# First chunk's x put in place by TensorE in a linear-attention and MLP kernel

## The chip, the cores and the metric

The kernel runs on one core of one Trainium2 chip. A core has TensorE (matrix products, written to PSUM), VectorE (DVE), ScalarE (ACT), GpSimd (POOL) and SyncE (SP, which here only issues DMA transfers). The engines run their own instruction queues in order and wait for one another through semaphores. The metric is device time of one execution in microseconds, the median of several runs.

## The reference

Two blocks, all in float32. The first is a recurrent attention over 4 sequences, 8 heads, 768 steps and 40 channels per head, with a state matrix of 40 x 40 per sequence and head. The second is an MLP over the 3072 tokens, with 320 channels in and out and 2048 hidden ones.

```python
for t in range(S):
    y[:, :, t] = einsum('bhd,bhde->bhe', r_t, state)
    Sa = einsum('bhde,bhe->bhd', state, a_t)
    state = state * w_t[:, :, None, :] - einsum('bhd,bhe->bhde', Sa, b_t)
    state = state + einsum('bhd,bhe->bhde', v_t, k_t)
x = y.transpose(0, 2, 1, 3).reshape(B * S, H * D)
h = x @ w_in
out = (h * sigmoid(1.702 * h)) @ w_out
```

## The kernel before

**Units and chunks.** The 768 steps are cut into 12 chunks of 64. A unit i is one chunk (i // 2) for two of the four sequences (i % 2), so there are 24 units; all 16 heads of a unit are worked on together as 64 x 64 blocks, four at a time on the four quadrants of TensorE's array. A product in float32 is two weight loads and two matmul instructions in the trace; every matmul of the kernel has the same line there, L301, the helper `mm`, so products are told apart by the PSUM tile that they write.

**A unit's steps, with the names of their PSUM tiles.** The decays w are turned into logarithms by ACT. `cum` and `cumc` sum them over time, once with time and once with channels on the partitions (`cumc` serves the first four units only, `i < BY_PE`; later units get these sums from a scan on DVE). Exponentials of the sums scale a, b and k. `N`, `A` and `RV` are the score products. From N, five levels (`ps_level`, called L0 to L4 of a unit here) invert a triangular matrix by repeated squaring. In the first four units each level is one group of products, then a copy of 128 x 768 out of PSUM (PT, line 794) and a transpose (EX, line 733). `Q` and `T21` (the tile ps_T) finish the inverse; `B0` and `B1` gather the known terms; `X` solves (its product with the mask is M, line 917); `y` gives the outputs and the new state. From unit 2 on, `zT` and `rz` bring in the state of the unit two before. The last step is x = y times the decay (line 962).

**How x reaches the MLP.** The output of a unit has 40 channels of each head on the partitions, two heads side by side; the MLP's up product wants 64 rows of the 320 channels at a time. Before the change x goes to DRAM in two transfers (`part_with`) and comes back in two (`get_back`, one for each half of the partitions), into the tile xT_all.

**The MLP.** For each chunk, `up` multiplies x by w_in in four groups of 10 tasks (group q needs the q-th of eight weight pieces), ACT applies the gate, and `down` multiplies by w_out. An up task is four products of 256 columns; the 64 x 64 tiles are in w_sb.

**The weights** come in as 64-bit floats, in eight pieces of 1.3 MB, four transfers each, and are turned into 32-bit ones on the chip: ACT (line 457, "rebased"), three DVE passes (lines 461, 465, 469) and one on POOL (line 473, "joined").

**The order of the work.** The function does not issue instructions as it goes. It adds some 2700 tasks to a plan, and a list written out in the file, ORDER, gives the order in which they are issued. Each word is a task's number, a letter for the engine (p TensorE, a ACT, d DVE, g POOL, s SyncE) and a digit: for tasks with a PSUM tile the bank pair, for SyncE's how many transfers may be under way (it waits for the one that many back; without a digit it does not wait). An engine therefore takes its tasks in the listed order, whatever else is ready. TensorE's first 54 tasks, up to the first up task, are (unit in parentheses):

```
cum(0) cumc(0) RV(0) A(0) N(0) cumc(1) cum(1) L0(0) B1(0) RV(1) N(1) L1(0) B0(0) L0(1) L2(0) L1(1) A(1) L3(0)
cum(2) cumc(2) L2(1) L4(0) L3(1) Q(0) T21(0) N(2) L4(1) X(0) B1(1) y(0) Q(1) B0(1) L0(2) T21(1) A(2) cumc(3)
cum(3) X(1) zT(2) y(1) N(3) L1(2) RV(2) rz(2) L0(3) L2(2) B0(2) zT(3) B1(2) L3(2) L1(3) L4(2) RV(3) A(3) up
```

## Time and profile before

| | |
|---|---|
| median of 3 runs | 682.24 us (681.4 to 682.74) |
| profiled execution | 679.49 us, of it span 677.7 us |
| TensorE matmul busy | 649.6 us, 96% of the span |
| DVE, ACT, POOL busy | 449.7, 329.1, 175.7 us |
| granted TensorE clock, mean | 0.994 |
| transfers | 69.74 MB, mean 103 GB/s |
| first up product starts | 66.48 us |

The span runs from the first to the last instruction; the profiled execution's time is 1.8 us longer, for what lies around it. In the groups and the timeline a line shows an engine, the tiles written and read, the shape and the number of instructions, and in brackets how long the engine stood idle before it and what ended that. Busy time of TensorE includes the latency of products that stand alone, so a busy TensorE is not always one at its peak.

### The profile page before, as it was taken

Reading aid. Unit: us, or ns where it says so; the run is one execution under the profiler, and the core shown is the slowest. Engines: PE = TensorE matmul, PEld = TensorE weight load, DVE = VectorE, ACT = ScalarE, POOL = GpSimd, SP = SyncE. Lnnn points to the kernel's source line nnn. Section 1 sums busy time; section 2 is a strip of 40 time slices with the busy share of each in tenths; the row PEclk is TensorE's granted clock in tenths of the full one; section 3 lists DMA queues with packets and bytes.
Section 4 is the critical chain, followed back from the end, with each engine's and each line's share of the span. In section 5 each row is a group of like instructions: output and inputs, shape, how many; then the busy total and the mean of one; then the engine's idle time right before and its main releaser. Section 6 shows DMA issues by size and latency. Waiting matters only on the chain.

```text
span 677.7 us, 42447 instructions
## 1 busy us (share of the span) xinstructions
PE 649.6 (96%) x19616; PEld 568.7 (84%) x19616; DVE 449.7 (66%) x916; ACT 329.1 (49%) x681; POOL 175.7 (26%) x201
## 2 busy tenths in 40 slices
PE   5777999999999999999999999999999999999997
PEld 4667787787999997888888899999889798799896
DVE  5777779777867668757776687868656766675001
ACT  3676745634564655654545445455344454263010
POOL 6541443324123123123113211322411421300000
PEclk9979999999999999999999999999999999999999
DMA  6875753415324314432404513513412411200200
GB/s 208 295 255 160 226 172 97 129 42 152 107 64 131 94 58 124 114 107 65 124 14 131 149 35 108 155 33 107 140 38 62 130 53 45 69 15 14 60 13 21
DMA packets 35473, 69.74 MB, mean 103 GB/s; under 512 B 5472, under 2 KB 14816, under 8 KB 35296
## 3 DMA queue, kind: packets, MB, share of 16 engines
q1 hardware_dynamic: 35216, 66.99, 32.9%
q8 instruction: 154, 2.52, 1.6%
q14 instruction: 23, 0.19, 0.1%
q10 hardware_dynamic: 80, 0.04, 0.0%
HBM read 59.15 MB, written 7.86 MB: 99 GB/s over the span
## 4 chain that ended last, share of the span: by engine, by line
PE 88%; DMA 6%; DVE 2%; issue 1%; SPq 1%; ACT 1%; DVEq 0%; ACTq 0%
PE ps_up L301 31%; PE ps_down L301 29%; PE ps_level L301 8%; PE ps_y L301 5%; PE ps_B L301 4%; PE ps_X L301 2%; PE ps_N L301 2%; PE ps_rz L301 1%; PE ps_RV L301 1%; PE ps_A L301 1%; PE ps_zT L301 1%; SPq L331 1%; DMA w_sb<-in_w_in 1%; PE ps_cum L301 1%; PE ps_T L301 1%
## 5 line engine op out<-in xcount | busy, mean ns | idle before, releaser
L301 PE MATMUL ps_up<-xT_all,w_sb 64*64 64x256 f32 x3840 | 253.3, 377 | 2.1 <-issue 1.3
L301 PE MATMUL ps_down<-w_sb,g 64*64 64x320 f32 (+1 forms) x3200 | 241.5, 419 | 0.2 <-ACT zr L879 0.2
L301 PEld LDWEIGHTS ps_up<-xT_all,w_sb 64*64 64x64 f32 x3840 | 170.8, 133 | 18.8 <-issue 2.1
L301 PEld LDWEIGHTS ps_down<-w_sb,g 64*64 64x64 f32 x3200 | 142.5, 133 | 31.6 <-issue 0.4
L1000 ACT ACTIVATE g<-ps_up 128x1024 f32<-128x1024 f32 x48 | 49.2, 1025 | 46.3 <-PE ps_up L301 45.8
L719 POOL TENSOR_TENSOR EX<-ES,quads 128x512 f32<-128x512 f32 x30 | 39.7, 1324 | 116.4 <-DVE ES L712 77.7
L761 ACT COPY W<-ps_level 128x512 f32<-128x512 f32 x56 | 32.8, 585 | 67.7 <-PE ps_level L301 66.0
L301 PEld LDWEIGHTS ps_level<-W,EX 64*64 64x64 f32 x2560 | 60.0, 134 | 5.4 <-DVE T L840 0.2
L763 DVE TENSOR_TENSOR E<-two,ps_level 128x256 f32<-128x256 f32 x80 | 33.1, 415 | 36.5 <-ACT W L761 32.3
L301 PE MATMUL ps_level<-W,EX 64*64 64x64 f32 (+1 forms) x2560 | 56.8, 217 | 0.0
L717 ACT ACTIVATE EX<-ES,quads 128x256 f32<-128x256 f32 x82 | 37.2, 501 | 31.9 <-DVE ES L712 31.3
L629 POOL TENSOR_TENSOR ak<-ak,FT 128x512 f32<-128x512 f32 x17 | 23.0, 1353 | 77.2 <-DMA ak<-in_ak 54.4
L301 PEld LDWEIGHTS ps_level<-PT,EX 64*64 64x64 f32 x1280 | 30.7, 138 | 11.5 <-DVE EX L733 3.3
L301 PE MATMUL ps_level<-PT,EX 64*64 64x64 f32 (+2 forms) x1280 | 32.5, 234 | 6.9 <-DVE EX L733 5.0
L712 DVE STREAM_TRANSPOSE ES<-E 128x256 f32<-128x256 f32 x80 | 35.3, 443 | 4.4
L301 PE MATMUL ps_y<-RV,kh 64*64 64x104 f32 (+1 forms) x768 | 35.4, 247 | 0.9 <-DVE M L917 0.9
L301 PE MATMUL ps_y<-M,bh 64*64 64x104 f32 (+1 forms) x768 | 35.5, 247 | 0.7 <-DVE M L917 0.5
L901 ACT COPY B<-ps_B 128x416 f32<-128x416 f32 (+1 forms) x35 | 17.2, 493 | 34.4 <-PE ps_B L301 34.2
L301 PEld LDWEIGHTS ps_y<-RV,kh 64*64 64x64 f32 x768 | 29.6, 133 | 3.2 <-DVE M L917 1.5
L917 DVE TENSOR_TENSOR M<-ps_X,later 128x832 f32<-128x832 f32 (+1 forms) x24 | 23.9, 995 | 10.2 <-PE ps_X L301 10.0
L301 PE MATMUL ps_B<-RV,A 64*64 64x104 f32 (+1 forms) x768 | 29.2, 252 | 0.8 <-issue 0.8
L637 POOL TENSOR_TENSOR kh<-time,G 128x320 f32<-128x320 f32 x18 | 16.2, 901 | 51.2 <-PE ps_y L301 34.6
(133 smaller groups left out, 1099.0 us busy)
## 6 DMA issues: line engine op xcount, KB each, us to landing
ak<-in_ak SPq DMA_DIRECT2D x48, 160.0 KB
rv<-in_rv SPq DMA_DIRECT2D x48, 160.0 KB
time<-in_time SPq DMA_DIRECT2D x24, 320.0 KB
xT_all<-x_dram SPq DMA_DIRECT2D x48, 160.0 KB
wc<-in_wc SPq DMA_DIRECT2D x20, 264.0 KB
logw<-in_w SPq DMA_DIRECT2D x24, 160.0 KB
RV<-in_v SPq DMA_DIRECT2D x24, 160.0 KB
b<-in_b SPq DMA_DIRECT2D x48, 80.0 KB
```

The lines of the kernel that those rows point to most:

```text
L301: nc.tensor.matmul(o, lhsT, rhs, start=start, stop=True, skip_group_check=True)
L331: begun.append(queue.dma_start(dst, src).ins)
L629: plan.add(R, {"DVE": 690.0, "POOL": 1270.0, "sbuf": True}, lambda t: of(t.engine).tensor_mul(ahT(), ahT(), FT_of(i)), reads=T("ak", "FT") ...
L637: plan.add(R + 4, {"POOL": 870.0, "DVE": 490.0, "sbuf": True}, lambda t, n=n, dst=dst: of(t.engine).tensor_mul(dst(i)[:, :, :D], by_head(t ...
L712: plan.add(rank, dve(256), lambda t: nc.vector.transpose(ES(n), source(t)), writes=[key("ES", n, 6)], **reads)
L717: nc.scalar.activation(dst[:, :, h], ES(n), ACT.Copy, scale=quads[:, h, :1])
L719: of(t.engine).tensor_mul(dst, ES(n).unsqueeze(2).to_broadcast([128, 8, 2, 32]), quads.unsqueeze(1).to_broadcast([128, 8, 2, 32]))
L761: plan.add(rank, any2(512), lambda t: copy(t.engine)(tiles_of(W(n + 1)), blocks(psum(t, ""), 64)), writes=[key("W", n + 1, 5)], pair=pair)
L763: plan.add(rank, dve(256), lambda t: nc.vector.tensor_sub(tiles_of(E(n + 1)), every(two32, [128, 2, 4, 32]), blocks(psum(t, ""), 64)[:, :, ...
L901: plan.add(R, any2(4 * wide), lambda t: copy(t.engine)(dst(), some(psum(t, "")[:, :, :208])), writes=[("Bv", i)] if x and c > 0 else T("B" ...
L917: plan.add(R + 1, dve(8 * wide), lambda t: nc.vector.tensor_tensor(M_of(i)[:, :, :wide].rearrange("p (j b) n -> p b j n", b=2), some(psum( ...
L1000: plan.add(-45, {"ACT": 1030.0, "table": "gelu"}, lambda t: nc.scalar.activation(g_of(c * NQ + q).rearrange("p m r n -> p r m n"), psum(t, ...
```

## The change

For the two units of the first chunk x no longer goes through DRAM. TensorE multiplies it by a selection matrix (`first_sel`, 128 x 128, one product of 512 columns) for four of the five groups of 64 channels, and by four shifted slices of a second one (`rest_sel`) for the last, which accumulate four products of 128 columns; one copy brings the 640 columns from PSUM into xT_all. The two matrices are built at the start by a new task, `selections`. The channels of x and the rows of w_in get a new order, in all chunks; in the later chunks x still goes through DRAM, with four transfers back in place of two. For the first two units y times the decay is two DVE operations instead of four.

For the first four units the decays come in a copy in which each head has 64 columns (40 and 24 ones), 256 KB in place of 160, and `cumc` takes two heads at a time: 8 products with 128 columns of weights in place of 16 with 64. Three small memsets on POOL go.

ORDER is new throughout. TensorE's first 54 tasks are now (xp is the selection):

```
cumc(0) cum(0) N(0) A(0) cumc(1) cum(1) RV(0) L0(0) B0(0) N(1) L1(0) B1(0) L0(1) L2(0) A(1) L1(1) RV(1) L3(0)
cumc(2) cum(2) L2(1) L4(0) L3(1) Q(0) T21(0) L4(1) X(0) Q(1) N(2) y(0) B0(1) B1(1) cumc(3) cum(3) T21(1) L0(2)
xp(0) L1(2) X(1) N(3) A(2) y(1) zT(2) rz(2) RV(2) L2(2) xp(1) zT(3) B1(2) L0(3) L3(2) B0(2) L1(3) L4(2) up
```

SyncE's queue is in a new order too. Adding up the sizes of its transfers, the point by which each has been asked for is, in MB:

| landed with | before | after |
|---|---|---|
| b(0) / ak(0) | 1.31 / 0.82 | 0.75 / 1.08 |
| rv(0) | 1.15 | 2.49 |
| rv(1) | 2.62 | 5.44 |
| w(2) | 2.79 | 6.03 |
| last of weight 1 | 6.23 | 10.23 |
| rv(2) | 7.37 | 11.64 |
| last of weight 3 | 9.83 | 13.72 |

Up to the first up task in the list, DVE has 67 tasks before and 74 after, ACT 60 and 53, POOL 14 and 15, SyncE 54 and 48. The diff, with the two lists left out:

```diff
@@ ORDER: 2709 words replaced by 2710 @@
...
@@ -352,6 +352,7 @@
     make_identity(nc, full)
     ident = single("ident", [128, 64])
     nc.vector.tensor_add(ident, full[:, :64], full[:, 64:])
+    first_sel, rest_sel = single("first_sel", [128, 128]), single("rest_sel", [128, 132])
     one32, two32 = single("one32", [128, 32]), single("two32", [128, 32])
     nc.vector.tensor_add(one32, ident[:, :32], ident[:, 32:])
     nc.vector.tensor_add(two32, one32, one32)
@@ -372,9 +373,7 @@
         select(edges[q], ALU.is_gt, 0, 1, -1.0)
         select(edges[p.start + MID:p.stop], ALU.is_gt, -MID, 1, 0.0)
     incl = edges[:, 1:]
-    logw_t = several("logw", [128, DM + 24])
-    for t in logw_t:
-        nc.gpsimd.memset(t[:, DM:], 0.0)
+    logw_t = several("logw", [128, DM])
 
     quads, within = single("quads", [128, 2, 32]), single("within", [128, 2, 32])
     nc.gpsimd.memset(quads, 0.0)
@@ -493,12 +492,13 @@
     ak_of, b_of, rv_of = lambda i: ak_t[i % 2], lambda i: b_t[i % 2], lambda i: rv_t[i % 2]
 
     RV_of = lambda i: buf("RV", i, [128, 13, 8, 8])
-    logw_of = lambda i: logw_t[i % 3][:, :DM]
+    logw_of = lambda i: logw_t[i % 3] if i >= BY_PE else apart(i).rearrange("p (h d) -> p h d", h=H)[:, :, :D]
 
     wc_of = lambda i: buf("wc", i, [128, 2, 8 * 33])
+    apart = lambda i: wc_of(i).rearrange("p n h -> p (n h)")[:, :H * 64]
 
     def load_w(i):
-        for name, of, src, n in (("wc", wc_of, wc_d, 528), ("logw", logw_of, w_d, DM))[i < BY_PE:]:
+        for name, of, src, n in (("wc", wc_of, wc_d, 528), ("logw", logw_of, w_d, DM)) if i >= BY_PE else (("wc", apart, apart_d, H * 64),):
             plan.add(-2 if i == 2 else 10 * i - 30, {"SP": 350.0}, lambda t, of=of, src=src: transfer(t, of(i), src[i]),
                      writes=[(name, i)], size=128 * n * 4)
 
@@ -535,7 +535,7 @@
                 nc.scalar.activation(wc_of(i), wc_of(i), ACT.Ln)
             nc.scalar.activation(logw_of(i), logw_of(i), ACT.Ln)
         plan.add(10 * i - 30, {"ACT": 1000.0 if i >= BY_PE else 470.0, "table": "exp"}, go,
-                 reads=[("logw", i)] + ([("wc", i)] if i >= BY_PE else []) + ([("exps", i - 2)] if i > 1 else []), writes=[("log", i)])
+                 reads=[("wc", i)] + ([("logw", i)] if i >= BY_PE else []) + ([("exps", i - 2)] if i > 1 else []), writes=[("log", i)])
 
         def sums(t):
 
@@ -550,20 +550,20 @@
         R = 10 * i - 9
 
         def by_time(t):
-            ps, lw = psum(t, "ps_cum"), logw_of(i)
+            ps, lw = psum(t, "ps_cum"), logw_of(i) if i < BY_PE else logw_of(i).rearrange("p (h d) -> p h d", h=H)
             for n in (1, 0):
                 for b in BITS:
                     u = b ^ n
-                    mm(ps[HALF[u], b, :160], incl[HALF[b]], lw[HALF[b], n * 160:(n + 1) * 160], True)
-        plan.add(R, pe((1, 160)), by_time, reads=T("log"), uses=T("logw"), room=T("G"), writes=T("cum"), pair=("cum", i))
+                    mm(ps[HALF[u], b, :160].rearrange("p (h d) -> p h d", d=D), incl[HALF[b]], lw[HALF[b], 4 * n:4 * n + 4], True)
+        plan.add(R, pe((1, 160)), by_time, reads=T("log"), uses=T("logw") if i >= BY_PE else T("wc"), room=T("G"), writes=T("cum"), pair=("cum", i))
 
         def by_channel(t):
 
             ps = psum(t, "ps_cumc")
             for u, f in product(BITS, BITS):
-                for b, e in QUARTERS:
-                    o, h = (2 * u + f) * 65, head(e, f, b, u) * D
-                    mm(ps[HALF[e], b, o:o + 65], logw_t[i % 3][HALF[b], h:h + 64], edges[HALF[b]], o == 0)
+                for b in BITS:
+                    o, h = (2 * u + f) * 65, head(0, f, b, u)
+                    mm(ps[:, b, o:o + 65], apart(i)[HALF[b], 64 * h:64 * h + 128], edges[HALF[b]], o == 0)
 
         def exp_of_product(t):
             tables(t)
@@ -579,7 +579,7 @@
                     nc.scalar.activation(ends[:, n, b], sums[:, b, :, 64 * n].rearrange("p (u f) -> p u f", u=2), ACT.Exp, scale=2.0 * n - 1.0)
 
         if i < BY_PE:
-            plan.add(R, pe((4, 65)), by_channel, reads=T("log"), uses=T("logw"), room=T("FT", "GT"), pair=("cumc", i))
+            plan.add(R, pe_wide((4, 65)), by_channel, reads=T("log"), uses=T("wc"), room=T("FT", "GT"), pair=("cumc", i))
 
         def exp_channel(t):
             tables(t)
@@ -958,15 +958,24 @@
             x = x_of().rearrange("p (n f) b t -> p n b f t", f=2)
             for u, b in product(BITS, BITS):
                 at = slice(4 * u + 2 * b, 4 * u + 2 * b + 2)
-                y = both(i)[:, at, :64] if c > 0 else part(t)[:, u, 2 * b:2 * b + 2, :64]
-                of(t.engine).tensor_mul(x[:, b ^ u, b], y, FT_of(i)[:, at])
-        if c > 0:
-            plan.add(R + 6, {"DVE": 1200.0, "POOL": 2300.0, "sbuf": True}, decayed, reads=T("y", "FT"), uses=T("rz"), writes=T("x"))
-        else:
-            plan.add(R + 6, {"DVE": 1000.0}, decayed, reads=T("FT"), writes=T("x"), pair=("y", i))
-
-
-        rows = lambda: drams[i].rearrange("(e d j) n -> e d (j n)", e=2, d=D)
+                of(t.engine).tensor_mul(x[:, b ^ u, b], both(i)[:, at, :64], FT_of(i)[:, at])
+
+        def first_x(t):
+
+            x = x_of().rearrange("p (u f) b t -> p b u f t", f=2)
+            y, FT = (v.rearrange("p u (b f) t -> p b u f t", f=2) for v in (part(t)[:, :, :, :64], FT_of(i).rearrange("p (u j) t -> p u j t", u=2)))
+            for b in BITS:
+                nc.vector.tensor_mul(x[:, b, ::1 - 2 * b], y[:, b], FT[:, b])
+
+        def chosen(t):
+
+            ps = psum(t, "ps_xT")
+            nc.tensor.matmul(ps[:, 0], first_sel, x_of().rearrange("p j b t -> p (j b t)"), start=True, stop=True, skip_group_check=True)
+            for j in range(4):
+                nc.tensor.matmul(ps[:, 1, :128], rest_sel[:, 3 - j:131 - j], x_of()[:, j].rearrange("p b t -> p (b t)"),
+                                 start=j == 0, stop=True, skip_group_check=True)
+
+        rows = lambda: drams[i].rearrange("(d e j) n -> e d (j n)", e=2, d=D)
 
         def part_with(t):
             if i not in drams:
@@ -976,9 +985,19 @@
 
         def get_back(t):
             for h in HALF:
-                transfer(t, xT_of(c)[h, p].rearrange("q k n -> q (k n)"), drams[i].rearrange("(q k) n -> q (k n)", q=64))
-        plan.add(-50, {"SP": 700.0}, part_with, reads=T("x"), writes=T("xd"), size=DM * 512)
-        plan.add(-50, {"SP": 700.0}, get_back, reads=T("xd") + ([("weight", raws.index("x"))] if c in (1, 2) else []), writes=[("xT", c), ("xs", (c, p))], size=2 * DM * 512)
+                transfer(t, xT_of(c)[h, p, :4].rearrange("q k n -> q (k n)"), drams[i][:256].rearrange("(q k) n -> q (k n)", k=4))
+                transfer(t, xT_of(c)[h, p, 4], drams[i][256:])
+        if c > 0:
+            plan.add(R + 6, {"DVE": 1200.0, "POOL": 2300.0, "sbuf": True}, decayed, reads=T("y", "FT"), uses=T("rz"), writes=T("x"))
+            plan.add(-50, {"SP": 700.0}, part_with, reads=T("x"), writes=T("xd"), size=DM * 512)
+            plan.add(-50, {"SP": 2200.0}, get_back, reads=T("xd") + ([("weight", raws.index("x"))] if c in (1, 2) else []),
+                     writes=[("xT", c), ("xs", (c, p))], size=2 * DM * 512)
+        else:
+            plan.add(R + 6, {"DVE": 800.0}, first_x, reads=T("FT"), writes=T("x"), pair=("y", i))
+            plan.add(R + 7, {"PE": 1740.0, "instr": 20}, chosen, reads=T("x") + [("sel", 0)], pair=("xp", i))
+            plan.add(R + 7, any2(640), lambda t: copy(t.engine)(
+                xT_of(c)[:, p].rearrange("q k n -> q (k n)"), psum(t, "").rearrange("p r n -> p (r n)")[:, :640]),
+                     writes=[("xT", c), ("xs", (c, p))], pair=("xp", i))
 
 
     g_of = lambda n: buf("g", n, [128, 2, 2, 256])
@@ -1043,6 +1062,16 @@
         for p in BITS:
             down(p)
 
+    def selections(t):
+
+        of(t.engine).memset(first_sel, 0.0)
+        of(t.engine).memset(rest_sel, 0.0)
+        first = first_sel.rearrange("p (h d e) -> p h d e", h=2, e=2)
+        rest = rest_sel[:, 3:131].rearrange("p (h d e j) -> p h d e j", h=2, e=2, j=4)
+        for e in BITS:
+            for to, cols in (first[HALF[e], :, :, e], slice(0, 32)), (rest[HALF[e], :, :, e, 0], slice(32, D)):
+                of(t.engine).tensor_copy(to, ident[HALF[e], cols].unsqueeze(1).to_broadcast([64, 2, cols.stop - cols.start]))
+    plan.add(0, {"POOL": 1600.0, "DVE": 900.0}, selections, writes=[("sel", 0)])
     for i in range(3):
         load_w(i)
     for i in range(2):
@@ -1117,7 +1146,7 @@
         return n.reshape(*t.shape[:2], 2, 8 * 33)
 
 
-    order = [d + D * (e + 2 * j) for e in range(2) for d in range(D) for j in range(H // 2)]
+    order = [q // 2 + D * (q % 2 + 2 * k) if k < 4 else 32 + q // 8 + D * (q // 4 % 2 + 2 * (q % 4)) for q in range(64) for k in range(5)]
     def pieces(x):
 
         x = x.reshape(4, -1, *x.shape[1:]).transpose(0, 2, 1, 3)
@@ -1127,10 +1156,14 @@
     w_in = pieces(w_in.reshape(8, 128, 640))
     w_out = pieces(np.asarray(moe_w_out).reshape(16, 128, 320))
 
+    by_time = time_tile(w, False)
+    apart = np.ones((4, 128, H, 64), np.float32)
+    apart[..., :D] = by_time[:4].reshape(4, 128, H, D)
     arrays = {
         "in_time": np.ascontiguousarray(np.stack([time_tile(k, True), time_tile(b, True)], 2)),
         "in_v": beside(v),
-        "in_w": time_tile(w, False),
+        "in_w": by_time,
+        "in_apart": apart.reshape(4, 128, H * 64),
         "in_wc": halves(channel_tile(w, "e", "ubf")),
         "in_ak": np.ascontiguousarray(np.stack([channel_tile(a, "e", "ubf"), channel_tile(k, "e", "ubf")], 2)),
         "in_b": channel_tile(b, "e", "ubf"),
```

## The prediction

> **What bounds the kernel now.** I read the page's slices first, then the windows table, then the timeline of TensorE up to the first up product, then SyncE's issues. Slices of the whole span, 16.9 us each:
>
> ```profile
> PE   5777999999999999999999999999999999999997
> ...
> PEclk9979999999999999999999999999999999999999
> ```
>
> TensorE is full from the fifth slice on and has room only in the first four. The windows table gives that in us (window, length, then busy time of PE, PEld, DVE, ACT, POOL, granted clock, DMA share, GB/s):
>
> ```profile
> 10.00:20.00 10.00, 7.48 (x233) 6.73 (x229) 5.96 (x10) 2.98 (x11) 2.50 (x2) 1.00 0.80 255
> ...
> 30.00:40.00 10.00, 7.31 (x237) 6.53 (x239) 7.50 (x14) 7.52 (x23) 5.85 (x3) 0.75 0.93 311
> ...
> 60.00:70.00 10.00, 8.04 (x300) 7.07 (x304) 7.73 (x13) 6.58 (x15) 2.96 (x1) 1.00 0.50 146
> ...
> 120.00:640.00 520.00, 518.21 (x15848) 456.14 (x15844) 356.52 (x758) 253.09 (x511) 122.69 (x133) 1.00 0.30 87
> ```
>
> From 120 to 640 us only 1.8 us of 520 are idle; before the first up product some 21 of 66.5 are. So the end is set by how soon TensorE reaches that product with the same work behind it. The timeline (start, length) shows the steps on the way that I time below:
>
> ```profile
> 11.71 1.13 PE L301 MATMUL ps_N<-b,ak 40*64 40x64 f32 x32 [0.82 <-DVE b L631]
> ...
> 42.00 0.41 PE L301 MATMUL ps_y<-RV,kh 64*64 64x104 f32 x8 [0.91 <-DVE M L917]
> ...
> 64.82 0.67 PE L301 MATMUL ps_level<-PT,EX 64*64 64x32 f32 x32 [0.84 <-DVE EX L733]
> ...
> 66.02 0.65 PE L301 MATMUL ps_A<-ak 40*64 40x64 f32 x32
> 66.48 2.48 PE L301 MATMUL ps_up<-xT_all,w_sb 64*64 64x256 f32 x40
> ```
>
> N(0) starts at 11.7 because it waited for b and its product; y(0) at 42.0; L4(2), the last level of unit 2, at 64.8. Up then follows A(3) without idle time: **no wait for x shows there**. SyncE's issues say why: x left for DRAM late and came back just in time.
>
> ```profile
> 44.63 0.66 SPq L331 DMA_DIRECT2D x_dram<-x  x2
> ...
> 56.67 0.84 SPq L331 DMA_DIRECT2D x_dram<-x  x2
> 61.39 1.09 SPq L331 DMA_DIRECT2D xT_all<-x_dram  x2
> ```
>
> Unit 1's x is written by 53.3, and is asked back only at 61.4.
>
> **What stands ahead of the first up product.** Both orders put 54 TensorE tasks there, the same ones but for two: RV(3) and A(3) move behind it (0.47 us each in stream, starts 65.55, 66.02, 66.48), and the two selections come ahead. So the work behind is 677.7 - 66.5 = 611.2 us before and 612.1 after, and the change gains only if the first up product starts before 65.6.
>
> **The walk to it.** I go through the new order queue by queue, with durations from rows: a level 0.88 us of TensorE in stream (61.98 to 62.86), 0.25 more until its last result; ACT's PT copy 0.80 and DVE's transpose 0.71, one after the other, since DVE's EX waited 7.7 us in six waits on ACT's PT; X 0.71, M 1.02, y 1.5; a DVE pass over a weight 0.8, ACT's 1.42, POOL's 2.97. Bytes arrive at 240 GB/s up to 14 us (rows 190 and 255 in the first two windows) and at 300 from there (291, 311). Behind each step stands its start before.
> - The first load is 256 KB in place of 160: at the 275 GB/s of 2 to 4 us that is 0.4 us, and with a weight piece beside it up to 0.8. The logarithm starts at 3.5 (3.2), but cumc now leads cum, so the exponentials start at 4.75 (5.6).
> - b(0) and ak(0) now stand first in SyncE's queue (0.75 and 1.08 MB against 1.31 and 0.82), landed by 6.2. b, a and k are scaled by 8.2: N(0) at 7.5 (11.7).
> - RV(0) stands ahead of L0(0) and needs rv(0), 2.49 MB, 12.0: L0(0) 12.5 (14.9).
> - L1(0) is no longer behind RV(1): 15.6 (19.8). RV(1) holds L3(0) to its 5.44 MB: 22.9 (26.9). cumc(2) holds L4(0) until w(2) has landed at 24.3 and ACT took its logarithm: 26.9 (30.8).
> - Four crossed copies of 0.44 on DVE, then Q, T21, X(0): 32.0 (38.6). M, then y(0): 34.6 (42.0).
> - L0(2) 37.8 (45.2), the first selection 38.7 to 40.4. ACT's first pass over weight 1 stands ahead of exp(3) and of the PT copy for L1(2); its last piece is at 10.23 MB, 38.3. L1(2) 43.3, X(1) 44.2 (48.4), y(1) 46.3 (49.5).
> - zT, rz, L2(2) 50.3; the second x on DVE waits behind two weight passes, selection 51.2 to 53; L3(2) 54.9, L4(2) 59.7 (64.8), held by DVE (a scan pair, shift of weight 1, EX, PT). Weight 1 is joined at 57.8. First up: **60.4**.
>
> The walk has no hand-offs: the chain of waits shows "issue" pieces of 0.02 to 0.06 us, some twenty on this path, so 0.8. It also runs at full clock. Before, the granted clock was 0.50 from about 35 to 41.8, behind 32 to 36 us where PE was busy 1.95 of 4; PE's 5.4 busy us in that stretch cost about 2.7 extra. The new order has two such thin stretches, 27.8 to 33.6 (2.7 busy of 5.8) and 40.4 to 43.3 (none). I take half of one dip, 1.3, with 0 to 5.4 as bounds. First up: 60.4 + 0.8 + 1.3 = 62.5, that is 3.1 before the 65.6 of no change. The Trainium skill (TensorE: Matmul & The Clock Gate, Part 1) says a window of some 3.4 us without activity halves the clock. The trace's dip of 6.8 us is two such windows, but came after a half busy stretch, not an empty one; by the rule neither stretch would cost a dip, since the empty one lasts 2.9 us, and the sum would be 1.3 us better.
>
> **The parts and their price.**
> - Selection: one product of 512 columns and four of 128 on the whole array. Up products take 0.43 us for 256 columns on four quadrants at once, so 0.86 + 0.86 = 1.7 each, 3.4 in all, counted in the walk. No row shows a 128 x 128 product: if the ten weight loads each take twice the 133 ns of a 64-column one and nothing hides them, 2.7 each, 2 us more in all; less than 1.7 is excluded, since the columns must stream. I take 1.7. Behind each waits only TensorE's next level. The Trainium skill (TensorEngine Tiling (Array Packing), Key Properties) says that a change of tiling mode drains TensorE. No row here shows one; if each of the four changes around the selections exposed the 0.3 us by which an up product's 377 ns exceeds its 54 ns in stream, the sum would be 1.2 us worse.
> - Channel sums: 8 products of twice the width for 16; half as many run at once, so 0.44 us stays; 0.4 to 0.9 by the same two ends, twice in thin places.
> - x: two DVE products over 256 columns for four over 128, 0.8 for 0.88; its copy 0.8 once on DVE, once on ACT. Four DRAM transfers of each unit's x go (4 x 0.35 us of SyncE, 0.98 MB in all), and with them SyncE's wait of 3.8 us for x_dram and 2.2 for x.
> - Selection matrices: six small operations on POOL, between 17.4 and 19.0, where before it idled from 17.0 to 22.9; nothing if that holds, else kh(1) is late by what is over, and it is wanted only at y(1).
> - Later chunks: two more SyncE issues per unit, 0.36 to 0.56 each, 22 units, some 20 us over 580 in which SyncE has slack; x of a chunk could land 1 us later. I take nothing, 0 to 2 us.
> - The order from 100 us on: TensorE is 99.6% full and can't gain. I take nothing, 0 to 2 us lost.
>
> **Sum.** The profiled execution took 679.49 us, 677.7 of it span; 3.1 less is 674.6 of span, 676.4 in all. That execution lies 2.75 below the median of the runs, 682.24, so the same difference there gives 682.24 - 3.1 = **679.1**. A measurement can tell about 0.2%, 1.4 us.
>
> **Rivals.**
> - *No gain: both thin stretches halve the clock.* For it: the 35 us dip. Against: 18 to 22 us had 2.3 busy of 4 and the clock stayed 1.00. Price 5.4 for 1.3: first up at 66.6, 683.2. Chance 0.14.
> - *Slower: ACT waits for weight 1.* The new queue loads weight 1's last piece at 10.23 MB, before at 6.23, and ACT waits for it ahead of the exp(3) and PT copies. Each us that it lands after 38.3 is a us on L1(2), and from 4.4 us later on it decides. The transfers under way are held to three or four ahead of it, and 40 to 50 us moved only 217 GB/s. At 235 GB/s over 14 to 45 us it lands at 45: first up 69.2, 685.8. Against: 20 to 40 us ran at 300. Chance 0.16.
> - *Slower: x never was the wait.* Up follows L4(2) in both orders. If the new order brings L4(2) no earlier, 3.4 us of selections stand in the way: first up 66.5 - 0.9 + 3.4 = 69.0, 685.6. The point is y(0): it must start before about 39. Against: N(0) alone moves 4 us. Chance 0.13.
>
> The forecast keeps 0.57: faster 0.57, same 0.14, slower 0.29. Range: down to no dip and a bit less of DVE's hold, first up at 57.5: 674.1; up to the slower cases' 686.
>
> **What would show it.** Right: N(0) near 8, y(0) near 35, y(1) near 47, first up near 62, and equal work behind it. A first up near 66 with the clock at 0.5 twice is the first rival; L1(2) behind ACT's pass over weight 1 the second; y(0) at 40 or later the third. Selections over 2 us, new waits of ps_up for weights or x after 70 us, or idle time over 3 us between 120 and 640 would make me wrong in the parts.

## The result: 1.3% slower, and the profile after

The changed kernel takes 689.64 us, the median of 6 runs (687.5 to 693.2), against 681.66 us of the kernel before beside it: a ratio of 1.0131, 95% interval [1.0096, 1.0166]. The profiled execution took 689.39 us, of it span 687.7; the forecast for it was 676.4. The slices (tenths) and the windows of the profile after (length, busy time of PE, PEld, DVE, ACT, POOL, clock, DMA share, GB/s):

```profile
PE   6787999999999999999999999999999999999997
...
PEclk9899999999999999999999999999999999999999
```

```profile
10.00:20.00 10.00, 9.34 (x238) 8.63 (x235) 6.01 (x9) 4.20 (x14) 5.20 (x11) 1.00 0.91 288
20.00:30.00 10.00, 6.32 (x230) 5.26 (x225) 7.08 (x10) 4.69 (x8) 2.33 (x2) 0.93 0.75 244
30.00:40.00 10.00, 8.46 (x240) 7.42 (x242) 6.01 (x16) 4.72 (x14) 3.91 (x3) 0.73 0.82 253
...
60.00:70.00 10.00, 7.31 (x264) 6.99 (x265) 8.43 (x9) 4.72 (x7) 4.77 (x2) 0.83 0.21 72
120.00:640.00 520.00, 514.87 (x15720) 451.37 (x15716) 360.08 (x771) 239.60 (x493) 127.75 (x143) 1.00 0.29 86
```

TensorE is fuller than before from 10 to 20 us, as meant, then thin at 20 to 30, and its clock is below 1.00 in two places, not one. The last line is the part that I had given no loss: 5.1 us idle between 120 and 640 us, before 1.8. The timeline of TensorE on the way to the first up product:

```profile
8.69 1.19 PE L301 MATMUL ps_N<-b,ak 40*64 40x64 f32 x30 [1.89 <-DVE ak L629]
...
28.06 1.07 PE L301 MATMUL ps_level<-PT,EX 64*64 64x96 f32 x32 [3.31 <-DVE w_sb L464]
...
42.20 0.41 PE L301 MATMUL ps_y<-RV,kh 64*64 64x104 f32 x8 [0.17 <-DVE QT L828]
...
48.32 1.13 PE L973 MATMUL ps_xT<-x,first_sel 128*128 128x512 f32 x2 [0.64 <-ACT wch L579]
49.28 1.05 PE L975 MATMUL ps_xT<-x,rest_sel 128*128 128x128 f32 x8
...
65.82 0.79 PE L301 MATMUL ps_B<-RV,A 64*64 64x104 f32 x15 [2.69 <-DVE B L904]
...
69.77 0.39 PE L301 MATMUL ps_up<-xT_all,w_sb 64*64 64x256 f32 x2
```

Up starts at 69.77, not at 62.5. N(0) is early, 8.69 for 11.71, but y(0) is where it was, 42.20 for 42.00. Two long stops stand out. The 2.69 us at 63.1 have a plain cause, in the timeline of DVE and POOL:

```profile
60.53 0.70 DVE L543 TENSOR_TENSOR_SCAN wc<-starts,wc 128x264 f32<-128x264 f32 x1
61.14 3.42 DVE L544 TENSOR_TENSOR_SCAN wc<-starts,wc 128x264 f32<-128x264 f32 x1
```

```profile
60.69 3.31 POOL L472 TENSOR_TENSOR w_sb<-w_sb 128x1280 int32<-128x1280 int32 x1 [8.82 <-DVE w_sb L464]
```

The second of two equal scans lasts until POOL's joining of weight 1 is over, 3.42 us for 0.70, and the copy of B1(2) stands behind it on DVE. The Trainium skill (GPSIMD Engine Reference, Specifications) says that POOL shares its SBUF interfaces with DVE, with contention for DVE instructions that have two SBUF inputs; the scan has two, and the trace agrees.

The 3.31 us ahead of L3(0) are put down to a DVE pass over a weight, but L3(0) reads nothing of it, and its inputs were done by 24.86. What fits is TensorE's own instructions. They come by DMA, on a queue of their own (packets, MB, share of 16 engines' span):

```profile
q8 instruction: 154, 2.52, 1.6%
```

That is 154 packets of 16 KB, 256 recorded TensorE instructions each (a weight load and a matmul are two, and its semaphore instructions count). One packet started at 25.74 and landed at 26.67, and L3(0) began 1.39 us later; it is instruction 961. Counting through both traces, nearly all stops that no engine's work explains lie at instruction 193 + 256 k, 1.25 to 1.6 us after a packet landed: TensorE had run out. Nowhere in these two do packets start less than 3.3 us apart (3.21 is the least in any run). In the waits from 120 to 640 us these stops are the "issue" lines (total, times, longest), the changed kernel first, then the kernel before:

```profile
PE ps_B L301 <- issue: 2.0, 3, 1.3
PE ps_y L301 <- issue: 0.8, 1, 0.8
PE ps_level L301 <- issue: 0.6, 1, 0.6
PE ps_RV L301 <- issue: 0.6, 1, 0.6
```

```profile
PE ps_up L301 <- DMA xT_all<-x_dram: 0.6, 1, 0.6
PE ps_up L301 <- issue: 0.3, 1, 0.3
```

In the sum: the first up product came 7.3 us later than forecast, and 687.7 - 69.77 = 617.9 us lie behind it, 5.8 more than the 612.1 forecast; 13.1 together, and 689.39 is 13.0 above 676.4.

### The profile page after: what moved, and what is told of

Read it like the earlier page. It is cut to its first block, busy times and chain, and to the rows that moved or that the text cites. A ratio compares the mean times of both kernels' runs of the same rounds, so it can differ in the third digit from the quotient of the medians.

```text
span 687.7 us, 42361 instructions
## 1 busy us (share of the span) xinstructions
PE 660.4 (96%) x19572; PEld 580.4 (84%) x19572; DVE 455.4 (66%) x936; ACT 309.5 (45%) x643; POOL 179.8 (26%) x213
## 4 chain that ended last, share of the span: by engine, by line
PE 88%; DVE 6%; DMA 2%; issue 2%; ACT 2%; SPq 0%; DVEq 0%; ACTq 0%
PE ps_down L301 29%; PE ps_up L301 29%; PE ps_level L301 9%; PE ps_y L301 5%; PE ps_B L301 4%; PE ps_X L301 2%; PE ps_RV L301 2%; PE ps_N L301 1%; PE ps_A L301 1%; PE ps_rz L301 1%; PE ps_cum L301 1%; PE ps_zT L301 1%; DVE EX L733 1%; DMA ak<-in_ak 1%; PE ps_Q L301 1%
## 5 line engine op out<-in xcount | busy, mean ns | idle before, releaser
L301 PE MATMUL ps_up<-xT_all,w_sb 64*64 64x256 f32 x3840 | 247.0, 377 | 0.0
L301 PE MATMUL ps_down<-w_sb,g 64*64 64x320 f32 (+1 forms) x3200 | 235.8, 419 | 0.8 <-DVE T L840 0.4
L301 PEld LDWEIGHTS ps_up<-xT_all,w_sb 64*64 64x64 f32 x3840 | 173.8, 133 | 17.5 <-issue 1.8
L301 PEld LDWEIGHTS ps_down<-w_sb,g 64*64 64x64 f32 x3200 | 150.5, 133 | 33.6 <-issue 1.5
L719 POOL TENSOR_TENSOR EX<-ES,quads 128x512 f32<-128x512 f32 x33 | 42.8, 1300 | 142.7 <-DVE ES L712 102.6
L761 ACT COPY W<-ps_level 128x512 f32<-128x512 f32 x49 | 28.6, 584 | 73.6 <-DVE E L763 43.0
L301 PE MATMUL ps_level<-PT,EX 64*64 64x64 f32 (+2 forms) x1280 | 35.6, 243 | 5.5 <-DVE w_sb L464 3.3
L301 PEld LDWEIGHTS ps_level<-PT,EX 64*64 64x64 f32 x1280 | 33.1, 145 | 9.1 <-DVE w_sb L464 3.5
L629 POOL TENSOR_TENSOR ak<-ak,FT 128x512 f32<-128x512 f32 x18 | 24.7, 1371 | 47.8 <-DMA ak<-in_ak 38.8
L1048 DVE TENSOR_TENSOR ob<-ob,ps_down 128x320 f32<-128x320 f32 (+1 forms) x25 | 11.7, 467 | 37.1 <-ACT ob L1046 36.8
L807 ACT COPY Tc<-ps_level 32x64 f32<-32x64 f32 x86 | 17.4, 202 | 30.8 <-DVE Tc L807 14.4
```

The source lines that it names most:

```text
L301: nc.tensor.matmul(o, lhsT, rhs, start=start, stop=True, skip_group_check=True)
L629: plan.add(R, {"DVE": 690.0, "POOL": 1270.0, "sbuf": True}, lambda t: of(t.engine).tensor_mul(ahT(), ahT(), FT_of(i)), reads=T("ak", "FT") ...
L719: of(t.engine).tensor_mul(dst, ES(n).unsqueeze(2).to_broadcast([128, 8, 2, 32]), quads.unsqueeze(1).to_broadcast([128, 8, 2, 32]))
L761: plan.add(rank, any2(512), lambda t: copy(t.engine)(tiles_of(W(n + 1)), blocks(psum(t, ""), 64)), writes=[key("W", n + 1, 5)], pair=pair)
L807: copy(t.engine)(dst, src[:, u, :, f])
L1048: plan.add(-45, dve(wide), lambda t: nc.vector.tensor_add(ob(), ob(), psum(t, "")[:, 1, :wide]), reads=[("ob", serial + n)], writes=[("out ...
```

## The experiments

The table has, for every kernel, the median and the ratio to the kernel before on the same chip, and from its one profile: the start of the first up product, the time from there to the last product's start, and the stops at packet ends ahead of and behind it. A stop counts where a step between two products is over 0.3 us, ends 1.1 to 1.75 us after a packet landed and lies within 16 instructions of 193 + 256 k; 0.05 us is taken off. Some waits of other kinds pass this test by chance: 2.9 us of old_stream's 8.6 are a wait for DVE ahead of ps_B, as in the changed kernel at 63.1; and a stop of 1.4 us at the limit of 1.75 is left out of new_order's 5.3. All times are in us.

| kernel | median | ratio [95%] | up | behind | stops |
|---|---|---|---|---|---|
| before, two profiles | 681.7 | | 66.5, 67.3 | 607.0, 606.1 | 2.7 + 3.6, 3.0 + 4.8 |
| after, two profiles | 689.6 | 1.0131 [1.0096, 1.0166] | 69.8, 71.3 | 613.7, 618.8 | 4.0 + 6.6, 5.6 + 9.9 |
| old_order | 691.0 | 1.0128 [1.0083, 1.0173] | 74.1 | 610.8 | 4.0 + 4.6 |
| new_order | 691.4 | 1.0153 [1.0084, 1.0222] | 71.5 | 614.0 | 5.3 + 7.1 |
| scan_late | 692.0 | 1.0141 [1.0087, 1.0194] | 67.3 | 619.1 | 3.1 + 11.1 |
| narrow_sums | 692.4 | 1.0150 [1.0097, 1.0204] | 70.0 | 615.3 | 9.3 + 6.2 |
| before_64 | 690.0 | 1.0089 [1.0044, 1.0133] | 72.1 | 608.6 | 8.7 + 4.1 |
| before_128 | 690.0 | 1.0112 [1.0039, 1.0186] | 77.8 | 606.9 | 7.4 + 4.4 |
| after_64 | 698.3 | 1.0216 [1.0172, 1.0261] | 72.5 | 616.9 | 1.2 + 7.6 |
| after_128 | 700.7 | 1.0253 [1.0215, 1.0292] | 77.2 | 617.0 | 0 + 7.1 |
| wide_only | 688.5 | 1.0109 [1.0077, 1.0140] | 71.1 | 611.6 | 4.2 + 4.7 |
| before_fast128 | 686.5 | 1.0061 [1.0033, 1.0088] | 70.5 | 612.0 | 7.2 + 4.4 |
| after_fast128 | 693.8 | 1.0186 [1.0134, 1.0238] | 70.8 | 621.7 | 2.9 + 8.8 |
| old_stream | 688.9 | 1.0143 [1.0119, 1.0167] | 70.8 | 612.0 | 8.6 + 5.9 |
| new_stream | 691.7 | 1.0175 [1.0149, 1.0201] | 70.2 | 613.5 | 5.4 + 5.0 |
| walk_fixed | 688.9 | 1.0128 [1.0096, 1.0160] | 70.2 | 615.6 | 3.5 + 10.4 |
| fixed_old_stream | 684.6 | 1.0063 [1.0034, 1.0091] | 69.4 | 609.5 | 5.2 + 3.1 |

**The order or the work?** old_order takes the changed kernel and lists its tasks as the kernel before does, with `140p2 141a2` (first selection and copy) ahead of y(1) and `195p1 196d1` ahead of zT(3). new_order takes the kernel before and lists its tasks as the changed kernel does; `part_with` and `get_back` of the first chunk stand on SyncE where x is ready.

> All of the changed work (selections, new channel order, channel sums two heads at a time) in the order of tasks of the kernel before; only the two selections with their copies are put in, the first ahead of the reading of unit 1, the second ahead of the second turned state of unit 3. Theory 'order' (the new order of tasks is what costs): the stretch behind the first up product is about 611 to 612 us again instead of 617.9; the first up product starts late, at 69 to 72 us, since two selections of 1.95 us and four channel sums 0.6 us longer now stand in TensorE's way there; in all 681 to 685 us. Theory 'work' (the new work is what costs, the four transfers of get_back in the stream above all): the stretch behind stays at 616 us or more and the time is 688 us or more.

> All of the work of the kernel before (x through DRAM, old channel order, channel sums one head at a time) in the new order of tasks; the four transfers of the first chunk's x are put in on SyncE where their x is ready. Theory 'order': 684 to 689 us, the stretch behind the first up product 615 to 618 us, and long TensorE waits with nothing seen to release them. Theory 'work': 679 to 683 us, the stretch behind 611 to 613 us.

Neither theory held: both are as slow as the whole change. In old_order up started at 74.1, later than either bound. Only the stretch behind divides them, 610.8 in the old order and 614.0 in the new. The parts' losses don't add up, either: the new order alone costs 1.5%, the work in the old order 1.3%, both together 1.3%.

**One part or one stop at a time.** scan_late moves the scans of unit 5:

```
- ... 31d 362a2 341d 300p3 ... 271d 469p0 ...
+ ... 31d 362a2 300p3 ... 271d 341d 469p0 ...
```

> The changed kernel with one VectorE task moved: the scans of unit 5's sums go behind the scans of unit 4's sums, away from GpSimd's joining of weight 1. Theory 'shared port' (the second scan waits out GpSimd's 3.3 us, and TensorE's 2.69 us wait at 63.1 us is that): the wait is under 0.5 us, the clock does not halve at 66 us, the first up product starts 2.5 to 3.5 us earlier (66.3 to 67.3 us) and the time is 686 to 687 us. Rival 'late weights or another VectorE operation takes its place': the first up product starts at 69 to 70 us as now, and the time stays at 689 to 690 us.

narrow_sums goes back to 64 columns in the channel sums:

```
-                for b in BITS:
-                    o, h = (2 * u + f) * 65, head(0, f, b, u)
-                    mm(ps[:, b, o:o + 65], apart(i)[HALF[b], 64 * h:64 * h + 128], edges[HALF[b]], o == 0)
+                for b, e in QUARTERS:
+                    o, h = (2 * u + f) * 65, head(e, f, b, u)
+                    mm(ps[HALF[e], b, o:o + 65], apart(i)[HALF[b], 64 * h:64 * h + 64], edges[HALF[b]], o == 0)
```

> The changed kernel with the channel sums again one head at a time (32 products of 64 columns for a unit, not 16 of 128), from the same operand. Two of the four sums lie on the chain of the start: at 0.6 us each for all four that TensorE gains at most 2.4 us, the time is 687 to 689 us. It also puts 32 more TensorE instructions (products and weight loads together) into each unit, 64 ahead of the 3.31 us stop at 24.7 us. Theory 'instruction supply' (the stop lies at recorded instruction 961, where a 16 KB packet of instructions ends): the stop is at instruction 961 again, now ahead of or inside the RV product of unit 1, 64 instructions of work earlier. Rival 'VectorE's weight passes hold up L3(0)': the stop stays right in front of the third squaring of unit 1, at instruction 1025.

The shared port held for its own wait: without the collision up starts at 67.3, 2.5 us earlier. The time did not follow. With every product behind it in the same order, scan_late falls back against the changed kernel by 6.0 us between 70 and 126 us, above all in steps of 0.53, 1.07, 0.79 and 0.52 us at packet ends and one of 2.18 us ahead of a ps_B product, which is put down to DVE. In narrow_sums the stop moved as the supply theory said, to ps_RV of unit 1 (23.10 to 24.83), and others came, 9.3 us of stops in the start; the narrower sums gained nothing.

**Unused instructions.** To move the packet ends against the work I put 32 or 64 products of 8 columns into a wait, ahead of RV(0) in the kernel before and of N(0) in the changed one:

```
+            for n in range(32 if i == 0 else 0):
+                mm(ps[HALF[0], 0, :8], ident[HALF[0]], edges[HALF[0], :8], True)
```

> The kernel before with 32 tiny products (64 TensorE instructions with their weight loads) of which nothing is used, put in at 6 to 8 us, where TensorE waits for a load; nothing else is changed. They move every later piece of work by 64 instructions against the ends of the 16 KB packets in which TensorE's instructions come (256 recorded instructions each; in the traces so far TensorE's unexplained stops all lie at instruction 193 plus a multiple of 256). Theory 'packet phase' (what the kernel before has and every version of it so far has lost is a good fit of the bursts of short products to these ends): the stops are at the same instruction numbers and so at other work, and the time rises by 3 to 10 us, to 685 to 692 us. Rival 'only order and work count': the products cost nothing in that wait, and the time is 681 to 683 us.

> The same with 64 tiny products, 128 instructions, half a packet. 'Packet phase': 685 to 692 us, with the stops at other work again. Rival: 681 to 684 us (some 2 us of tiny products in a wait of 2 to 3 us).

> The changed kernel with 32 tiny unused products in TensorE's wait ahead of N of unit 0 (6.8 to 8.7 us), 64 instructions. 'Packet phase': the 3.31 us stop ahead of the third squaring of unit 1 moves with the packet's end to the RV product of unit 1 or ahead of it, and the sum of all stops at packet ends changes by 2 us or more in either direction; the time is anywhere from 684 to 693 us. Rival: the stop stays ahead of the third squaring and the time at 689 to 690 us.

> The same with 64 tiny products, 128 instructions. 'Packet phase': as for 64, with the stop another 64 instructions earlier, in the squarings of unit 0 or A of unit 1; 684 to 693 us. Rival: 689 to 691 us.

These four were badly made. A float32 product is two recorded ones, so they moved the ends by 128 and 256 instructions, and as all went through one quarter into one place each took 107 ns (which of the two did it was not separated): N(0) came 3.2 and 10 us late in the kernel before, 4.6 and some 11 in the changed one. Their times prove nothing. What they do show is that the stop ahead of L3(0) went, as the sum of stops in the start fell to 1.2 and 0.

before_fast128 and after_fast128 are the same test with 64 recorded products over four quarters and eight places (`for n in range(8) for b, e in QUARTERS`), 1.86 and 1.83 us, all inside the wait:

> The kernel before with 64 recorded tiny products (128 instructions) in TensorE's wait at 5.6 to 7.9 us, now spread over the four quarters and eight places, so that one no longer waits for the one before (107 ns each in the first try, 1 to 2 us for all of them here). If the order of tasks alone decides, 682 to 684 us with the stretch behind the first up product at 607 to 609 us to the last product; if the phase of the packets decides, stops of the walk at other places that sum to 5 us or more (2.7 us before), and 685 to 690 us.

> The changed kernel with the same 128 instructions in TensorE's wait ahead of N of unit 0 (6.8 to 8.7 us). If the 3.31 us stop ahead of the third squaring of unit 1 is a wait for instructions, it is gone or at other work, N of unit 0 starts within 0.5 us of 8.7 us, and the first up product starts 2 to 5 us earlier (65 to 68 us); the stretch behind it stays at 613 us or more (its order is the same), so 685 to 690 us. If the stop is a wait for VectorE, it stays, and so does the time, 689 to 691 us.

This was clean. In before_fast128 N(0) starts at 11.61 and y(1) at 49.76 (11.71 and 49.54 without), so the products cost nothing there; but the stops of the start sum to 7.2 us for 2.7, and up starts 4.0 us later. The clock is no rival for that: the records have 0.5 for 6.6 us ahead of up, 6.8 in the kernel before. In this execution another 4.9 us were lost behind up, of them at most 1.8 to the clock, which stayed at 0.5 until 74.1; but it is the slowest of six, 1.9 us above their median, and the median is 0.6% over the kernel before. **Half a packet of instructions that do nothing and hide in a wait cost some 4 us.** In the changed kernel the stop ahead of L3(0) is gone (a packet end costs 1.6 us at 20.7 instead) and y(0) starts at 38.47, 3.7 us earlier; yet up starts at 70.8, and the time of 693.8 is above the 685 to 690 expected. The timelines of TensorE and ACT:

```profile
25.73 0.89 PE L301 MATMUL ps_level<-PT,EX 64*64 64x96 f32 x32
...
46.33 1.13 PE L975 MATMUL ps_xT<-x,first_sel 128*128 128x512 f32 x2 [2.62 <-ACT wch L579]
```

```profile
43.56 1.35 ACT L456 ACTIVATE w_sb<-w_sb 128x1280 f32<-128x1280 f32 x1 [1.74 <-DMA w_sb<-in_w_in]
44.81 0.65 ACT L575 ACTIVATE FT<-ps_cumc 128x256 f32<-128x256 f32 x2
```

L3(0) now follows without a stop. But ACT waits for weight 1's last piece, which lands at 43.5 and not at 38.3, with unit 3's exponentials behind it, and TensorE waits 2.62 us for those: the second rival of the forecast.

**The supply by itself.** supply leaves out the recurrence and both layers. TensorE does 2048 recorded short products that wait for nothing, and 2048 more while weights come in:

```
+    def short(n, rhs):
+        for k in range(n):
+            for b, e in QUARTERS:
+                mm(ps[HALF[e], b, k % 8 * 64:k % 8 * 64 + 64], ident[HALF[b]], rhs[HALF[b], :64], True)
```

> Neither the recurrence nor the two layers are computed: TensorE does 2048 recorded short products (64x64 by 64 columns, four quarters in turn, with a weight load each) that wait for nothing, once with no load under way and then 2048 more while 21 MB of weights come in; then zeros are written out. Theory 'instruction supply': a packet of 256 instructions cannot come more often than every 3.3 us (the shortest interval in the traces so far), so 128 products take 3.3 us, 26 ns each and not the 15.5 ns that the same products take in the stream; with the load under way 4 us or more for a packet, 31 ns or more for a product. Rival 'the stops are waits for other engines that the profile does not show': 15 to 16 ns for each product in both stretches, packets every 2 us.

Two windows of its profile, the quiet and the loaded part, and what its instruction queue brought in each:

```profile
10.00:60.00 50.00, 27.91 (x1713) 26.03 (x1708) 0.00 (x0) 0.00 (x0) 0.00 (x0) 1.00 0.02 4
70.00:110.00 40.00, 24.14 (x896) 22.95 (x896) 0.00 (x0) 0.00 (x0) 0.00 (x0) 0.59 1.01 422
```

```profile
q8 instruction: 13, 0.21, 1.7%
```

```profile
q8 instruction: 6, 0.10, 1.0%
```

Quiet, 1713 products took 50 us: 29 ns each for the 15.5 that such products take in the stream, 3.7 us for a packet. Loaded, 896 took 40 us: 45 ns each, with packets about 6 us apart. Half the clock can't explain that, since 15.5 ns would become 31. So the supply is a ceiling of its own, and with these transfers under way it is lower. Both rates are slower than the 26 and 31 ns that were expected at the least interval.

**The channel sums alone.** wide_only is the kernel before with the sums of the change (`apart`, 128 columns), nothing else:

> The kernel before, in its own order, with one part of the change alone: channel sums two heads at a time from the new operand (256 KB for unit 0's first load, not 160 KB); x goes through DRAM as before. By the sums' own rows (0.6 us more each, two of four on the chain of the start, and 0.4 to 0.8 us for the larger first load): the first up product starts 1.6 to 3.2 us later and the time is 684 to 686 us, with N of unit 0 at 12.5 to 13.5 us. Rival 'fewer instructions': with 128 TensorE instructions less in the walk its stops at packet ends get shorter, and the time is 680 to 683 us.

The price by rows failed at both ends: N(0) came at 12.09, 0.4 later and ahead of the 12.5 expected, but up is 4.6 us later, for 1.6 to 3.2, and 4.6 us more lie behind it, where no sum is. One thing on the way is the clock. Its records have 0.5 for 13.7 us ahead of up, for 6.8 and 3.4 in the two profiles of the kernel before; at half clock TensorE's work takes at most twice as long, so 6.8 us more of it are worth up to 3.4 us.

**The order of the stream alone.** old_stream is the changed kernel up to its first up product and then the remaining tasks in the order before; new_stream is the counterpart with the work before. walk_fixed has after_fast128's products and moves `29a` behind `335a2`, `30d` behind `348d`, `32d` behind `141d2` and `341d` behind `271d`; fixed_old_stream is that with the order before from the first up product on.

> The changed kernel to its first up product, task for task; from there on the remaining tasks in the order of the kernel before. Theory 'order of the stream': the stretch from the first up product to the last product is 607 to 611 us instead of 613.7, and the time 683 to 686 us (first up product at 69.8 us as in the changed kernel). Rival 'the work, or whatever the start leaves behind, makes the stream longer': 613 us or more behind, 688 to 691 us.

> The counterpart: the kernel before, with its own work, to its first up product; from there on the remaining tasks in the changed kernel's order. 'Order of the stream': first up product at 66.5 us, 612 to 618 us behind it instead of 607, 685 to 690 us. Rival: 607 to 609 us behind, 681 to 683 us.

> The changed kernel with the three stops of its start taken out: 128 unused instructions ahead of N of unit 0 (moves the packet end off the third squaring of unit 1), ScalarE's rebasing of weight 1 and the two VectorE passes behind it put later, behind the exponentials of unit 3 (ScalarE waited 1.7 us for that weight), and the scans of unit 5 behind those of unit 4. If these stops are what kept the start from its forecast of 62.5 us, the first up product starts at 64 to 67 us (the sums' 0.6 us each remain); with the new order behind it the gain is partly given back (614 to 620 us to the last product) and the time is 684 to 689 us. If each stop is only replaced by the next wait, the first up product stays at 69 to 71 us.

> The same start, and from the first up product on the order of the kernel before. If the start gains 3 to 5 us and the order of the stream is what costs behind it: first up product at 64 to 67 us, 607 to 611 us behind, 676 to 683 us. If starting earlier only brings TensorE sooner to the ends of its packets and to weights that are not ready: 611 us or more behind and 683 to 688 us.

At an equal start the changed order is 6.5 us longer behind it with the old work (613.5 to 607.0) and 6.1 with the new (615.6 to 609.5). The times of the last pair differ too, by ratios whose intervals don't touch. old_stream, though, is no faster than the changed kernel, and its gain of 1.7 behind up is within what one profile of the changed kernel differs from another. new_stream's up also came 3.7 us later than before, with the same TensorE tasks ahead of it; the clock is the nearest cause, 0.5 for 17.1 us of it in three stretches, against 6.8, which is worth up to 5.1 us; the other engines' and SyncE's tasks around it are listed otherwise, and what set the dips off was not followed. The treated starts did not get better: with all three stops treated, up stays at 70.2 and 69.4. In walk_fixed a packet end still stopped TensorE for 2.58 us, now within a squaring, at 23.9. fixed_old_stream had none there (its 5.2 us of stops lie elsewhere) and ran at full clock from 22.1 us to its last product. Its y(0) came at 39.15, and behind it DVE is the fullest engine, with 9.55 of 10 us, which suggests it as the next limit (no run tested that):

```profile
50.00:60.00 10.00, 8.19 (x332) 7.09 (x322) 9.55 (x18) 5.64 (x9) 0.00 (x0) 1.00 0.56 178
```

**Scatter.** Each kernel profiled a second time:

> The kernel before, unchanged, profiled a second time. If executions of one program scatter in their start (new_stream's first up product came 3.7 us later with the same instructions ahead of it): first up product at 66 to 71 us, and the time 679 to 685 us. If they do not: 66.3 to 66.7 us, and new_stream's delay comes from something in its later order.

> The changed kernel, unchanged, profiled a second time. With scatter: first up product at 68 to 72 us, 612 to 617 us from it to the last product, the stops at packet ends at other places or of other lengths than in the first profile, 687 to 692 us in all. Without: 69.6 to 69.9 us, and the 3.31 us stop ahead of the third squaring of unit 1 again.

The kernel before repeats to 1 us in both parts. The changed one does not: up comes 1.5 us later, 5.1 us more lie behind it, with 9.9 us of stops for 6.6, and its 695.9 us are above all six runs of the result. The stop ahead of L3(0) is there again, 1.68 us of idle time for 3.31. So a difference of a few us between single profiles of the new order says little.

**What follows.** The loss behind the first up product belongs to the order. Seven profiles with the order before from start to end have 606 to 612 us behind up, 609.0 in the mean, with 4.4 us of stops; eight of the changed kernel and its variants in the new order have 614 to 622, 617.2 in the mean, with 8.5. Of those 8.2 us 0.9 are the two products that moved, 4.1 the stops and 1.5 other waits over 0.3 us; the last 1.7 lie in shorter steps and were not traced. new_order and new_stream, the old work in the new order, lie below the eight with 614.0 and 613.5, but still above all others. One reason for more stops can be counted in the traces: behind up, 2805 short products (all but up and down) stand in unbroken runs of over 64 in the new order, 1302 in the old; runs longer than a packet's 128 hold 160 and 0. Such a run takes 16 ns a product, 2 us a packet, and in no run did the next packet start sooner than 3.2 us. No run broke these runs up alone, so that they make the stops is argued and not shown; new_stream has them too, with only 5.0 us of stops behind up. No version beat the kernel before; of those with the changed work fixed_old_stream came nearest.

## Why the prediction was wrong

- **The walk** is the step that failed first: 62.5 forecast, 69.77 measured. It put TensorE's products one after another and asked only for data, engines and the clock, never for instructions. L3(0) was due at 22.9; TensorE was ready for it at 24.7 and began at 28.06. Up to y(0) the walk was 7.6 us too quick (34.6 against 42.20): 1.8 ahead of that stop, 3.4 in it, and 2.4 behind it, where 11.7 us became 14.1, much of them at half clock. That the stop is the packet's, and no engine's, is shown by after_fast128. From y(0) to up the walk's own 25.8 us came near the 27.6 measured, but by luck: 2.7 of these are a wait for DVE that it did not have.
- **The clock:** half a dip was counted, 1.3 us. The records show 0.5 from 28.6 to 35.5, behind the 3.31 us stop, and from 66.2 to 69.6, behind the 2.69 us wait. This is the first rival's mechanism, set off by stops that it did not name. The Trainium skill's rule of 3.4 us windows (TensorE: Matmul & The Clock Gate, Part 1) agrees with both lengths, two windows and one; its condition of a window without activity is not borne out, since the stops took 3.31 and 2.69 us. The walk also took full speed from the start. But up to 18.4 us, where the records begin, products take twice as long: 104.1 ns from one to the next in the channel sum at 11.3 us, 55.8 at 44.9; and in the kernel before 26.0 at 12.6 us, 13.8 at 47.3.
- **Channel sums** ("half as many run at once, so 0.44 us stays") was mis-sized: its products follow each other 55.8 ns apart at full speed, where those of the old sum come four at once, 13.8 apart; so the two row halves do not run at once, and a sum takes 1.04 us, and 1.98 at 11.3 us.
- **DVE's hold** left out that POOL can stop DVE: 2.7 us.
- **Selections** were right within the bounds: 1.95 us each (48.32 to 50.27), for 1.7. The draining that the Trainium skill (TensorEngine Tiling (Array Packing), Key Properties) tells of at a change of tiling mode was estimated at 1.2 us for both. They took 0.5 more than priced, and no run here shows whether that is a drain.
- **The order from 100 us on** ("0 to 2 us lost") is the other step that failed: 5.8 us in the first profile. That TensorE was 99.6% full was read as room for nothing to go wrong; it did not show that another order would be as full.
- **Later chunks' two more issues:** nothing to be seen; old_order has them and its 610.8 lies among the other old-order stretches.
- **The second rival** did not occur in the first profile: ACT took up weight 1 at 45.50 without a wait for its transfer. Its price was wrong by its own words: if a late weight decides only from 4.4 us on, 6.7 us cost 2.3 and not 6.7.
- **The third rival** named the sign: y(0) at 40 or later, up at 69.0, 685.6 us. The sign and the up product came as it said (42.20, 69.77), but not for its reason alone: when y(0) came at 38.5, up did not follow, and the second rival's wait for weight 1 appeared. All three rivals kept the stretch behind as it was, which is why 686.0 was too low an upper end.

## What to carry to other kernels

Before moving short products together, count TensorE's instructions: packets came 3.7 us apart at the best sustained rate here, so a long run that eats 256 faster stops, whatever the data do, and beside heavy transfers, at about 6 us a packet, sooner. A stop whose releaser makes no sense is checked against the instruction queue's packets first. Where one profile shows an almost full engine, a new order of the same work has more to lose than to win, and the order is worth testing alone, behind an unchanged start, before the work is changed.

## What the runs showed of the hardware

- TensorE's instructions come in 16 KB packets of 256, never under 3.2 us apart in the traces; bound by them alone (supply), one each 3.7 us, and about 6 us beside 422 GB/s of loads. It resumes 1.2 to 1.6 us after one lands, seldom later.
- A DVE scan with two SBUF inputs waited out a POOL operation, 3.42 us for 0.70.
- Products of 8 columns took 107 ns each through one quarter into one PSUM place and 29 ns over four quarters and eight places (1.86 us for 64).
